# First batch of a fused agent-attention and expert layer: queries moved behind the values, 320 instead of 384 units checked per token

## The chip, the cores and the metric

The kernel runs on one core of one Trainium2 chip. The metric is the device time of one launch in microseconds (us). Engines are named as in the profile: PE is TensorE (PEld its weight loads), DVE is VectorE, ACT is ScalarE, POOL is GpSimd, SP is SyncE, which here only issues DMAs.

## What is computed

The reference, cut to what matters (B = 4 batches, N = 11456 tokens, 49 agents, width 128, E = 8 experts with 1024 hidden units):

```python
def sm(a, b):                         # softmax of scaled scores
    s = scale * (a @ b.transpose(0, 2, 1))
    e = np.exp(s - s.max(-1, keepdims=True))
    return e / (e.sum(-1, keepdims=True) + 1e-09)
agent_v = sm(agents, k) @ v           # 49 x 128 for each batch
x = (sm(q, agents) @ agent_v).reshape(B * N, 128)
...
expert_idx = argmax(normalized(x) @ normalized(expert_emb).T / tau)
gate_w = softmax probability of the chosen expert
for e in range(E):                    # tokens of expert e
    h = np.maximum(x[mask] @ w1[e], 0.0)
    out[mask] = gate_w[mask, None] * (h @ w2[e])
```

## The kernel before, in words

Each batch is cut into 12 units of 128 tokens by up to 8 (the last unit is 96 by 2). A unit of keys, values or queries is one DMA of 512 KB into a ring of 11 buffers (`unit_load`, L134 to L153). SP issues the loads in a fixed order, and load number n waits until the unit in load n-11 has been used.

For a batch b the work is:
- **keys** (`k1_f32`, L363): PE transposes the unit (tile `fTp`, `pe_T` L346), ACT and DVE copy it out (`fT`), PE multiplies by the agents (`sp`), ACT keeps the scores (`s_u`), DVE holds a running maximum (`m_run`).
- **maximum** (`k_max`, L416): one maximum over all tokens for each agent, by a transpose (`mT`), a reduction and a broadcast (`mB`, `pm`).
- **values** (`k2_unit`, L385): DVE subtracts the maximum, ACT takes the exponential (`kd`), PE multiplies with the values (`avp`), DVE adds up (`avx`).
- **the chain** (`av_chain` L421 and `pick_expert` L471): `foldp` and `avT` give agent_v; `key` and `e0i` choose the expert that most tokens of the batch will take; SP reads that number and loads its two weight matrices (`w1s`, `w2s`, `load_expert` L653); `gp` gives the product G of weights and agent_v, 1024 units by 49 agents. The units are ranked by how far their 49 numbers differ in sign (`diag`, in the trace written into `sel`; `row`; `rank`), and a selection matrix (`sel`) places the first 256 (384 in the last batch) into `gh` and `gl`.
- **queries** (`q_unit`, L666): PE transposes the unit, multiplies by the agents (`sp`), DVE and ACT form the exponentials (`qe`, `e`), which come back transposed (`tt`; for the first four units by PE as `tp`, later by DMA), then `rtp` gives routing scores (`rtg`, `rt`, `qq`), which `route_group` turns into gates.
- **the expert layer** (`ffn_mm1`, `ffn_mm2`): the 256 placed units get the full two-layer product (`hp`, `hh`, `hl`, `yp`). Of the other units the sign is held to be the same for all tokens, so that they enter as one linear map (`lin`).
- **the check** (`proved`, L810): the next `FVS[b]` units in rank are checked token by token with one matmul `vp`, whose least value is taken by DVE (`vmin`) or whose negative part is summed by ACT (`vsum`, L824). All units behind these are covered by a bound on the token alone. A token that fails, or that belongs to another expert, is a stray (`mark_strays`): up to 3 per partition and 128 per batch are computed again in one pass per batch (`fix`), what is left is handled in passes of a loop at the end (`stray`).

Ahead of the first expert product, `first()` (L1210) writes batch 0 out by hand. Its list `ops` is: 12 key units, query units 0 and 1, the maximum, then 12 value units, with query units 2 and 3 and key units 0 and 1 of batch 1 put between them (`BETWEEN`). Then come the chain up to `gl` and the rest. After that a table of ticks lays batch b's expert products over the keys, values and queries of the batches to come, and a scheduler orders each engine's instructions (SP's order is as written).

Of the kernel before, what the change touches and what calls it, by code (L numbers as in the profile page):

```python
# [10 lines left out]
F32 = mybir.dt.float32  # L11
# [3 lines left out]
ALU = mybir.AluOpType  # L15
# [3 lines left out]
P = 128  # L19
# [10 lines left out]
def kernel(ctx: ExitStack, tc: tile.TileContext, q, k, v, agents, emb, tau, w1, w2, out):  # L30
# [7 lines left out]
    NMS = [2] * (B - 1) + [3]  # L38
    FVS = [3 * P] * (B - 1) + [4 * P]
    FW = 4 * P  # L40
# [41 lines left out]
    def pss(name):  # L82
        return ps_s.tile([P, 512], F32, name=name, tag="s")
# [186 lines left out]
    def setup():  # L270
# [39 lines left out]
        yield 2  # L310
        t_ = pss("embT")
        pe.transpose(out=t_[:, :E], in_=emb_sb, identity=ident[:E, :E])
# [8 lines left out]

    y_last, h_last = [], []
    x_slots, s_slots, d_slots, e_slots, t_slots, qe_slots = slots(XB), slots(NU), slots(len(kds)), slots(len(e16)), slots(TB), slots(LEAD)
# [99 lines left out]
    def av_chain(b, g):  # L423
        bt = batches[b]
        while not ready:
            yield 1
        psx = pss if ffn_at[0] else psh
        s = psx("foldp")
# [22 lines left out]
        pe.matmul(out=rp[:, :E], lhsT=bt.avT, rhs=enT, start=True, stop=True)  # L451
        pe.matmul(out=rp[:, E + 1 : RW], lhsT=bt.avT, rhs=bt.avT[:, :A], start=True, stop=True)
        bt.sg, bt.isg = yield from half_scale(total(sq, psx), 7, "sg")
# [13 lines left out]
        yield 4  # L467
        s = pss("avsT")
        pe.transpose(out=s[:A, :D], in_=bt.avT[:, :A], identity=ident)
        act.copy(av_all[:, b, :], s[:A, :D])  # L470

    def pick_expert(b, g):
# [5 lines left out]
        def psx(name):  # L478
            return (pss if ffn_at[0] else psh)(name)

# [36 lines left out]
        def col(nm, dt=F32):  # L517
            return sm.tile([P, NF], dt, name=nm, tag=nm)
# [35 lines left out]
        act.copy(gs_[0], gg)  # L554
        vec.tensor_tensor(out=gs_[1], in0=gg, in1=gs_[0], op=ALU.subtract)
        gmx = sm.tile([P, 2], F32, name="gmx", tag="gmx")
        dve.tensor_reduce(out=gmx[:, :1], in_=ga, axis=AX.XY, op=ALU.max, apply_absolute_value=True)
        yield g
        for h in range(2):
# [4 lines left out]
            yield g  # L564

        rank, more = col("rank"), col("more")
        for c in range(NF // 2):
# [12 lines left out]
        def placed(h, w):  # L580
            t_ = psx("placed")[:, :w]
            for c in range(NF):
                pe.matmul(out=t_, lhsT=gt16[:, h, c].rearrange("p h a -> p (h a)"), rhs=sel[:, c, :w],
                          start=(c == 0), stop=(c == NF - 1))
            return t_

        act.copy(gh, placed(0, FM))
        yield g
        dve.tensor_copy(gl, placed(1, FM))
        bt.gh, bt.gl = gh, gl  # L590
        yield g
        act.activation(w2x[:, :, 0], w2s, AF.Square, accum_out=sq[1])
# [73 lines left out]
    def q_unit(b, u, g):  # L666
# [6 lines left out]
        i = yield from take(x_slots)  # L673
        xT = pe_T(units["q", b, u], p, n)
        used("q", b, u)
# [528 lines left out]

    QF = 2
    BETWEEN = {1: ("q", 0, 2), 5: ("q", 0, 3), 8: ("k", 1, 0), 11: ("k", 1, 1)}
    NEXT = sum(x[0] == "k" for x in BETWEEN.values()) if B > 1 else 0
    AHEAD = LB - 2

    def first():  # L1210

        ops = [("k", 0, u) for u in range(NU)] + [("q", 0, u) for u in range(QF)] + [("m", 0, 0)]
        for u in range(NU):
            ops.append(("v", 0, u))
            if u in BETWEEN and BETWEEN[u][1] < B:
                ops.append(BETWEEN[u])
        X = {"k": k, "v": v, "q": q}
        loads = [o for o in ops if o[0] in X]
        li = 0
        q0 = []  # L1220
        for kind, b, u in ops:
            if kind in X:
                li += 1
                for o in loads[: li + AHEAD]:
                    while o not in units and len(ring) >= LB and ring[-LB][1] is None:
                        yield 1
                    unit_load(X[o[0]], *o)
            if kind == "k":
                if not hasattr(batches[b], "blks"):
                    k_start(b)  # L1230
                spawn(k1_f32(b, u))
            elif kind == "v":
                spawn(k2_unit(b, u, dve, (0, 1)))
            elif kind == "q":
                g = q_unit(b, u, (1, 0, 0, 1, 0) if u < QF else (1, 1, 1, 5, 1))
                if u == 0:
                    q0.append(g)
                    spawn(iter(lambda: next(q0[0]), None))
                else:
                    spawn(g)  # L1240
            else:
                kb = batches[0].blks[0]
                while kb.k1 < len(kb.us):
                    yield 1
                with tc.high_priority():
                    now_run(k_max(0, psh, 0))
            yield 1
        while batches[0].blks[0].k2 < NU or not ready:
            yield 1
        with tc.high_priority():  # L1250
            now_run(av_chain(0, 0))
            now_run(q0[0])
            q0[0] = iter(())
            while not hasattr(batches[0], "gl"):
                next(batches[0].pick)
        yield from batches[0].pick

# [156 lines left out]
```

## Time and profile before

| what | value |
|---|---|
| median of 3 runs | 865.67 us (864.28 to 867.6) |
| the profiled execution, own time | 861.1 us |
| its span | 859.3 us |
| mean granted TensorE clock | 0.939 of full speed |
| busy: PE, DVE, ACT, POOL | 90%, 74%, 55%, 35% |
| loaded and stored | 114.5 MB, mean 133 GB/s |

The profiled execution lies 4.6 us under the median of the runs. Its span runs from the first instruction to the last; 1.8 us of its time lie outside. The granted clock is shown as a share of full speed: 1.00 is 2.4 GHz and 0.50 is 1.2 GHz. A matmul of float32 operands leaves two records in the trace for each one in the program; a transpose leaves one.

### The profile page before, as it was taken

The numbers are of one execution on the slowest core, as the hardware profiler recorded it, in microseconds if no ns is written. First come the engines' busy times: TensorE is split into PE (matmuls) and PEld (weight loads), VectorE is DVE, ScalarE is ACT, GpSimd is POOL, SyncE is SP. The second block draws the span as 40 slices with busy tenths as digits, with TensorE's granted clock in tenths as the row PEclk, the third lists the DMA queues.
The fourth block names the chain that finished last, engine by engine and source line by source line (L and its number), as shares of the span: only waits on it lengthen the run. The fifth ranks groups of instructions, "written<-read, shape, count | busy, mean of one in ns | idle before, by whom it ended". The sixth has DMA issues, their size and how long they took to land. (4 is left out here: it accounts for less than half of the span.)

```text
span 859.3 us, 20983 instructions
## 1 busy us (share of the span) xinstructions
PE 771.5 (90%) x8158; PEld 647.7 (75%) x8158; DVE 636.1 (74%) x1576; ACT 475.7 (55%) x1191; POOL 303.8 (35%) x554
## 2 busy tenths in 40 slices
PE   8979469999998889989998979989995779999986
PEld 6978359988787687868987768878883657888765
DVE  5545586786666997967578976967686979887976
ACT  2434254675655835665557624766557436776662
POOL 4000221334603353553414353544522634334420
PEclk9969569999998999999999979999998989999998
DMA  8737106456417145855537143764342224521311
GB/s 332 216 103 263 58 1 214 136 154 207 146 60 241 71 116 153 250 167 159 184 76 224 46 132 104 210 186 132 88 132 56 75 56 109 150 79 42 101 46 57
DMA packets 126608, 114.50 MB, mean 133 GB/s; under 512 B 47541, under 2 KB 102921, under 8 KB 126507
## 3 DMA queue, kind: packets, MB, share of 16 engines
q1 hardware_dynamic: 113131, 89.58, 36.2%
q10 hardware_dynamic: 13120, 23.47, 7.4%
q8 instruction: 65, 1.06, 0.5%
q14 instruction: 36, 0.29, 0.1%
q0 software_dynamic: 256, 0.10, 0.1%
HBM read 79.14 MB, written 23.72 MB: 120 GB/s over the span
## 5 line engine op out<-in xcount | busy, mean ns | idle before, releaser
L941 DVE SCALAR_TENSOR_TENSOR hl<-hp,hh 128x512 f16<-128x512 f32 (+1 forms) x207 | 137.6, 668 | 40.9 <-ACT hh L940 40.1
L940 ACT ACTIVATE hh<-hp 128x512 f16<-128x512 f32 (+1 forms) x207 | 120.1, 584 | 82.6 <-PE hp L937 73.7
L824 ACT ACTIVATE vp<-vp,la 128x384 f32<-128x384 f32 (+1 forms) x224 | 130.1, 581 | 51.7 <-PE vp L821 34.3
L964 PE MATMUL yp<-w2p,hh 128*128 128x128 f16 (+1 forms) x810 | 154.9, 220 | 0.4 <-ACT hh L940 0.4
L965 PE MATMUL yp<-w2p,hh 128*128 128x128 f16 (+1 forms) x810 | 154.9, 220 | 0.0
L966 PE MATMUL yp<-w2p,hl 128*128 128x128 f16 (+1 forms) x810 | 151.2, 220 | 1.4 <-DVE hiv L216 1.0
L821 PE MATMUL vp<-vm,tt 128*128 128x384 f16 (+1 forms) x360 | 115.2, 342 | 6.9 <-ACT vp L824 2.8
L679 PEld LDWEIGHTS sp<-aT_all,fT 128*128 128x128 f32 x720 | 89.4, 196 | 7.9 <-issue 1.8
L964 PEld LDWEIGHTS <-hh 128*128 128x128 f16 (+1 forms) x810 | 81.3, 100 | 17.9 <-issue 1.4
L679 PE MATMUL sp<-aT_all,fT 128*128 128x49 f32 x720 | 91.1, 276 | 3.5 <-DVE hsc L212 1.4
L376 PEld LDWEIGHTS sp<-aT_all,fT 128*128 128x128 f32 x720 | 89.4, 196 | 5.0 <-DVE lin L615 2.4
L376 PE MATMUL sp<-aT_all,fT 128*128 128x49 f32 x720 | 90.1, 274 | 2.5 <-DVE lin L615 2.2
L966 PEld LDWEIGHTS <-hl 128*128 128x128 f16 (+1 forms) x810 | 79.8, 99 | 14.5 <-issue 2.5
L826 DVE TENSOR_REDUCE vmin<-vp 128x1 f32<-128x384 f32 (+3 forms) x136 | 78.7, 580 | 14.9 <-PE vp L821 14.5
L936 PE MATMUL hp<-tt,gh 128*128 128x512 f16 (+1 forms) x207 | 77.9, 376 | 10.4 <-ACT vp L824 8.1
L965 PEld LDWEIGHTS <-hh 128*128 128x128 f16 (+1 forms) x810 | 80.3, 99 | 8.5 <-issue 1.4
L358 DVE COPY fT<-fTp 128x512 f32<-128x512 f32 x88 | 60.0, 684 | 24.9 <-PE fTp L355 24.5
L937 PE MATMUL hp<-tt,gl 128*128 128x512 f16 (+1 forms) x207 | 78.0, 377 | 0.0
L360 ACT COPY fT<-fTp 128x512 f32<-128x512 f32 (+1 forms) x96 | 54.0, 564 | 29.5 <-PE fTp L355 29.4
L694 POOL TENSOR_TENSOR e<-qe,e 128x392 f16<-128x392 f32 (+1 forms) x44 | 38.0, 864 | 89.7 <-ACT e L693 88.6
L955 PE MATMUL yp<-lin,tt 128*128 128x128 f16 x720 | 66.5, 220 | 2.8 <-DVE ot L979 2.7
L773 POOL TENSOR_TENSOR nrm<-qq,half 128x16 f32<-128x16 f32 (+2 forms) x28 | 68.5, 2446 | 0.2
(330 smaller groups left out, 1644.8 us busy)
## 6 DMA issues: line engine op xcount, KB each, us to landing
kt<-in_k_dram SPq DMA_DIRECT2D x44, 512.0 KB, 5.9
qt<-in_q_dram SPq DMA_DIRECT2D x44, 512.0 KB, 4.4
vt<-in_v_dram SPq DMA_DIRECT2D x44, 512.0 KB, 4.9
out_dram<-ot ACTq DMA_DIRECT2D x88, 256.0 KB, 2.6
w1s<-in_moe_w_dram SPq DMA_DIRECT2D x8, 512.0 KB, 3.7
w2s<-in_moe_w_dram SPq DMA_DIRECT2D x8, 512.0 KB, 5.3
tt<-e SPq DMA_TRANSPOSE x44, 3.1
kt<-in_k_dram SPq DMA_DIRECT2D x4, 96.0 KB, 6.0
```

The source lines that it names most:

```text
L376: pe.matmul(out=s[:p, c * A : (c + 1) * A], lhsT=kT[:, c * p : (c + 1) * p], rhs=aT_all[:, b, :], start=True, stop=True)
L679: pe.matmul(out=s[:p, c * A : (c + 1) * A], lhsT=xT[:, c * p : (c + 1) * p], rhs=aT_all[:, b, :], start=True, stop=True)
L821: pe.matmul(out=z[:p, :FV], lhsT=tts[b, u][:, c * p : (c + 1) * p], rhs=bt.vm, start=True, stop=True)
L824: act.activation(z[:p, :FV], z[:p, :FV], AF.Relu, bias=bt.l[:p, at], scale=-1.0, accum_out=bt.vsum[:p, at])
L826: dve.tensor_reduce(out=bt.vmin[:p, at], in_=z[:p, :FV], axis=AX.X, op=ALU.min)
L936: pe.matmul(out=hp[:, :m], lhsT=bt.gh[:, fs], rhs=tt, start=True, stop=False)
L937: pe.matmul(out=hp[:, :m], lhsT=bt.gl[:, fs], rhs=tt, start=False, stop=True)
L940: h_last[:] = [act.activation(hh[:, :m], hp[:, :m], AF.Relu)]
L941: dve.scalar_tensor_tensor(out=hl[:, :m], in0=hp[:, :m], scalar=0.0, in1=hh[:, :m], op0=ALU.max, op1=ALU.subtract)
L964: pe.matmul(out=y, lhsT=hh[:, cs], rhs=wh, start=False, stop=False, skip_group_check=True)
L965: pe.matmul(out=y, lhsT=hh[:, cs], rhs=wl, start=False, stop=False, skip_group_check=True)
L966: y_last[:] = [pe.matmul(out=y, lhsT=hl[:, cs], rhs=wh, start=False, stop=last, skip_group_check=True)]
```

## The change

The first batch's order is now: 12 key units, maximum, 12 value units, the chain as far as `rp`; queries 0 and 1 are put behind `rp` on PE, queries 2 and 3 behind the start of the chain's second half. Batch 1's key units 0 and 1 go to the general plan (`NEXT = 0`). The chain's small products of batch 0 use the two output banks (`psy`) instead of the four hidden-layer banks. The maximum `gmx` and the low half `gs_[1]` are written later. In batches 0 to 2 the check covers 320 units and not 384.

```diff
-    FVS = [3 * P] * (B - 1) + [4 * P]
+    FVS = [P * 5 // 2] * (B - 1) + [4 * P]
...
-        t_ = pss("embT")
+        t_ = psy("embT")
...
-        psx = pss if ffn_at[0] else psh
+        psx = pss if ffn_at[0] else psy
...
-        pe.matmul(out=rp[:, E + 1 : RW], lhsT=bt.avT, rhs=bt.avT[:, :A], start=True, stop=True)
+        i = pe.matmul(out=rp[:, E + 1 : RW], lhsT=bt.avT, rhs=bt.avT[:, :A], start=True, stop=True)
+        if not ffn_at[0]:
+            p_last.append(i)
...
-        s = pss("avsT")
+        s = psx("avsT")
...
-        vec.tensor_tensor(out=gs_[1], in0=gg, in1=gs_[0], op=ALU.subtract)
-        gmx = sm.tile([P, 2], F32, name="gmx", tag="gmx")
-        dve.tensor_reduce(out=gmx[:, :1], in_=ga, axis=AX.XY, op=ALU.max, apply_absolute_value=True)
...
+        vec.tensor_tensor(out=gs_[1], in0=gg, in1=gs_[0], op=ALU.subtract)
         rank, more = col("rank"), col("more")
...
         bt.gh, bt.gl = gh, gl
+        dve.tensor_reduce(out=gmx[:, :1], in_=ga, axis=AX.XY, op=ALU.max, apply_absolute_value=True)
...
-        xT = pe_T(units["q", b, u], p, n)
+        with in_place(p_last):
+            xT = pe_T(units["q", b, u], p, n)
...
-    QF = 2
-    BETWEEN = {1: ("q", 0, 2), 5: ("q", 0, 3), 8: ("k", 1, 0), 11: ("k", 1, 1)}
-    NEXT = sum(x[0] == "k" for x in BETWEEN.values()) if B > 1 else 0
+    NEXT = 0
...
-        ops = [("k", 0, u) for u in range(NU)] + [("q", 0, u) for u in range(QF)] + [("m", 0, 0)]
...
+        k_start(0)
         for u in range(NU):
...
+            yield from fetch(u + 1 + AHEAD)
+            spawn(k1_f32(0, u))
+            yield 1
+        while batches[0].blks[0].k1 < NU:
+            yield 1
+        with tc.high_priority():
+            now_run(k_max(0, psy, 0))
+        for u in range(NU):
+            yield from fetch(NU + u + 1 + AHEAD)
+            spawn(k2_unit(0, u, dve, (0, 1)))
+            yield 1
+        yield from fetch(len(loads))
         while batches[0].blks[0].k2 < NU or not ready:
             yield 1
         with tc.high_priority():
             now_run(av_chain(0, 0))
-            now_run(q0[0])
-            q0[0] = iter(())
+        for u in range(2):
+            spawn(q_unit(0, u, (1, 0, 0, 1, 0)))
+        while len(tts) < 2:
+            yield 1
+        p_last.clear()
+        with tc.high_priority():
             while not hasattr(batches[0], "gl"):
                 next(batches[0].pick)
+        for u in range(2, LEAD):
+            spawn(q_unit(0, u, (1, 0, 0, 1, 0)))
         yield from batches[0].pick
```

Line numbers of the changed kernel differ by 2 or 3 from those of the kernel before (L562 becomes L561, L679 becomes L682, L715 becomes L718).

How the engines' order moves, at three places. First, PE from the last unit of keys to the first values (`qt` is a query unit, `vt` a value unit, `m` the running maximum). Before:

```order
L376 MATMUL sp<-aT_all,fT 96x49 x2
L679 MATMUL sp<-aT_all,fT 128x49 x8
...
L355 MATMUL fTp<-ident,qt 128x128 x5
L196 MATMUL mT<-ident,m_582 49x128
L355 MATMUL fTp<-ident,qt 128x128 x3
L679 MATMUL sp<-aT_all,fT 128x49 x4
L201 MATMUL mB<-ident,mTx 128x49
L679 MATMUL sp<-aT_all,fT 128x49 x4
L405 MATMUL avp<-vt,kd_152 64x129 x8
```

Now:

```order
L376 MATMUL sp<-aT_all,fT 96x49 x2
L196 MATMUL mT<-ident,m_527 49x128
L201 MATMUL mB<-ident,mTx 128x49
L312 MATMUL embT<-ident,emb_sb 128x8
L405 MATMUL avp<-vt,kd_152 64x129 x8
```

The two query units that stood around the maximum are gone from this place, and the values follow it directly; between the values, too, only `avp` is left.

Second, PE from the fold of the values to the ranking product `row` (left out are the transposes `tp` and the pairs `rtp`, 16 and 32 matmuls now, 16 `rtp` before). Before:

```order
L376 MATMUL sp<-aT_all,fT 128x49 x8
L431 MATMUL foldp<-fold,avx 128x49
...
L451 MATMUL rp<-enT,avT 128x8
L452 MATMUL rp<-avT 128x49
L222 MATMUL total<-avsq,ones 128x1
...
L522 MATMUL gp<-avT,w1s 128x49 x8
L222 MATMUL total<-wsq_1022,ones 128x1
L562 MATMUL row<-sel,ones 128x512 x2
```

Now:

```order
L451 MATMUL rp<-enT,avT 128x8
L452 MATMUL rp<-avT 128x49
L355 MATMUL fTp<-ident,qt 128x128 x16
L222 MATMUL total<-avsq,ones 128x1
L682 MATMUL sp<-aT_all,fT 128x49 x12
L471 MATMUL avsT<-ident,avT 49x128
L682 MATMUL sp<-aT_all,fT 128x49 x4
L524 MATMUL gp<-avT,w1s 128x49 x8
...
L355 MATMUL fTp<-ident,qt 128x128 x12
...
L682 MATMUL sp<-aT_all,fT 128x49 x12
L561 MATMUL row<-sel,ones 128x512 x2
```

The last eight `sp` of batch 1's keys no longer stand ahead of `foldp`; two query units stand between `rp` and `gp`, two more between `gp` and `row`.

Third, DVE between the mean of G and the matrix `diag` (written into `sel`) that `row` waits for. Before:

```order
L533 TENSOR_REDUCE mean<-gts 128x8
...
L536 TENSOR_REDUCE pw<-sel 128x8
...
L555 TENSOR_TENSOR gt_158<-gts,gt_158 128x16x49
L538 TENSOR_SCALAR pw<-pw 128x8
...
L550 TENSOR_TENSOR sel<-ident,key 128x1024
```

Now:

```order
L565 TENSOR_TENSOR gt_158<-gts,gt_158 128x16x49
L736 TENSOR_TENSOR rt<-rtp,qe 128x392
L542 RECIPROCAL pw<-pw 128x8
L772 TENSOR_REDUCE rmx<-rtg 128x8
L739 TENSOR_REDUCE qq<-rt 128x2x8
L358 COPY fT<-fTp 128x512
L544 TENSOR_TENSOR key<-key,pw 128x8
L736 TENSOR_TENSOR rt<-rtp,qe 128x392
L546 TENSOR_SCALAR key<-key 128x8
L739 TENSOR_REDUCE qq<-rt 128x2x8
...
L552 TENSOR_TENSOR sel<-ident,key 128x1024
```

Routing work of queries 0 and 1 and copies for queries 2 and 3 now stand between the steps of `key`.

## Rows read from the trace of the kernel before

**Rows 1.** Windows of the whole core. Columns: stretch in us, its length, busy us (and instructions) of PE, PEld, DVE, ACT, POOL, then granted clock, DMA share, GB/s.

```profile
20.00:42.00 22.00, 22.00 (x205) 22.00 (x205) 11.40 (x34) 8.64 (x18) 0.68 (x6) 1.00 0.74 218
50.00:60.00 10.00, 10.00 (x64) 9.32 (x61) 4.88 (x10) 4.78 (x9) 0.11 (x1) 0.50 0.26 65
68.00:86.00 18.00, 17.00 (x209) 15.19 (x205) 9.44 (x23) 7.90 (x15) 0.00 (x0) 0.99 0.86 290
96.00:117.00 21.00, 7.56 (x23) 4.98 (x24) 11.81 (x36) 10.07 (x18) 4.07 (x8) 0.50 0.01 3
124.00:800.00 676.00, 629.55 (x6859) 527.88 (x6859) 521.43 (x1246) 400.58 (x1031) 269.73 (x462) 0.97 0.45 133
```

**Rows 2.** The timeline from the last keys to the first values. Columns here and in the next three groups: start us, duration us, engine, line, operation, tile written <- tiles read, shapes, count of merged records, and in brackets the idle time before and what ended it.

```profile
41.96 0.46 PE L376 MATMUL sp<-aT_all,fT 128*96 128x49 f32 x4
43.72 0.82 DVE L419 TENSOR_REDUCE m<-m_run 128x49 f32<-128x392 f32 x1
51.30 0.42 PE L196 MATMUL mT<-ident,m 128*49 128x128 f32 x1
51.76 0.28 DVE L198 TENSOR_REDUCE mTx<-mT 49x1 f32<-49x128 f32 x1 [2.41 <-PE mT L196]
53.90 0.66 PE L201 MATMUL mB<-ident,mTx 49*128 49x49 f32 x2
55.44 1.48 ACT L399 ACTIVATE kd<-kd 128x392 f32<-128x392 f32 x3 [0.63 <-DVE kd L396]
56.36 3.71 PE L405 MATMUL avp<-vt,kd 128*64 128x129 f32 x32
```

**Rows 3.** The timeline: the same PE work at either clock, and the end of the values.

```profile
51.52 0.85 PE L355 MATMUL fTp<-ident,qt 128*128 128x128 f32 x3
52.16 1.81 PE L679 MATMUL sp<-aT_all,fT 128*128 128x49 f32 x8
63.05 1.99 PE L679 MATMUL sp<-aT_all,fT 128*128 128x49 f32 x16 [0.85 <-ACT fT L360]
125.34 1.06 PE L355 MATMUL fTp<-ident,kt 128*128 128x128 f32 x8
73.92 1.10 PE L405 MATMUL avp<-vt,kd 128*64 128x129 f32 x16
83.02 1.33 PE L405 MATMUL avp<-vt,kd 128*64 128x129 f32 x20 [0.19 <-issue]
```

**Rows 4.** The timeline of the chain from the fold to the sum of squares of the first weights.

```profile
86.40 0.39 PE L431 MATMUL foldp<-fold,avx 128*128 128x49 f32 x2
87.28 0.56 DVE L346 TENSOR_TENSOR m_run<-sp,m_run 128x392 f32<-128x392 f32 x1
89.67 0.64 PE L452 MATMUL rp<-avT 128*128 128x49 f32 x2
91.70 0.36 SPq L658 DMA_DIRECT2D w1s<-in_moe_w_dram  x1
95.51 3.65 PE L522 MATMUL gp<-avT,w1s 128*128 128x49 f32 x16 [2.27 <-DMA w1s<-in_moe_w_dram]
98.96 0.55 PE L222 MATMUL total<-wsq,ones 128*128 128x1 f32 x2
```

**Rows 5.** The timeline of the chain's second half, up to the first expert product, and query steps that now stand in it (the transposed copy `tt`, `rt`, `qq`).

```profile
106.52 3.75 PE L562 MATMUL row<-sel,ones 128*128 128x512 f32 x4 [7.01 <-DVE nkey L552]
110.93 1.28 DVE L568 TENSOR_SCALAR_CACHE_REDUCE sel<-sel,key 128x1024 f16<-128x1024 f32 x1 [4.47 <-ACT sel L563]
116.11 0.16 DVE L573 TENSOR_SCALAR rank<-more 128x4 f32<-128x4 f32 x1
121.64 0.41 DVE L589 CAST gl<-placed 128x256 f16<-128x256 f32 x1
124.09 0.38 PE L936 MATMUL hp<-tt,gh 128*128 128x512 f16 x1 [0.24 <-ACT fT L360]
50.48 1.01 ACT L700 COPY tt<-tp 128x1024 f16<-128x1024 f16 x1 [1.86 <-PE tp L699]
93.53 0.57 DVE L733 TENSOR_TENSOR rt<-rtp,qe 128x392 f32<-128x392 f32 x1 [1.22 <-ACT rtg L731]
94.20 0.97 DVE L736 TENSOR_REDUCE qq<-rt 128x16 f32<-128x784 f32 x1
52.40 0.69 DVE L358 COPY fT<-fTp 128x512 f32<-128x512 f32 x1 [0.36 <-PE fTp L355]
```

**Rows 6.** Groups of instructions by line with different shapes apart, whole span: count, busy us, mean ns of one, idle before. The check's matmul and ACT's pass over it.

```profile
L821 PE MATMUL vp<-vm,tt 128*128 128x384 f16 x264 | 80.6, 329 | 5.1 <-DVE vmin L826 2.2 <-ACT vp L824 1.8 <-DVE hl L941 0.8
L821 PE MATMUL vp<-vm,tt 128*128 128x512 f16 x88 | 31.9, 385 | 1.6 <-ACT vp L824 1.0 <-ACT vm L645 0.4
L824 ACT ACTIVATE vp<-vp,la 128x384 f32<-128x384 f32 x165 | 91.5, 555 | 37.9 <-PE vp L821 26.6 <-POOL la L805 8.8 <-PE yp L966 0.6
L824 ACT ACTIVATE vp<-vp,la 128x512 f32<-128x512 f32 x55 | 36.4, 661 | 9.4 <-PE vp L821 6.4 <-PE mB L201 2.4 <-POOL la L805 0.2
```

**Rows 7.** A window where batch 0's expert products end and batch 1's begin, columns as in rows 1.

```profile
290.00:300.00 10.00, 7.73 (x91) 6.28 (x90) 10.00 (x21) 7.94 (x21) 3.09 (x8) 1.00 0.07 26
```

**Rows 8.** The passes over strays: the writes of their answers (nanoseconds; first and last start in us), and the start of the pass that the last one ends.

```profile
L1075 POOL DMA_INDIRECT out_dram<-so,ix x4: 1114/1127/1131, 429.8 to 853.6; - x4
800.46 0.23 DVE L1101 TENSOR_SCALAR_CACHE_REDUCE ind<-cum,it 128x32 f32<-128x32 f32 x1
```

More of the change, by code (lines that the diff above doesn't have):

```diff
@@ L317 @@
     ready = []
-    y_last, h_last = [], []
+    y_last, h_last, p_last = [], [], []
     x_slots, s_slots, d_slots, e_slots, t_slots, qe_slots = slots(XB), slots(NU), slots(len(kds)), slots(len(e16)), slots(TB), slots(LEAD)
@@ L478, in psx @@
         def psx(name):
-            return (pss if ffn_at[0] else psh)(name)
+            return (pss if ffn_at[0] else psy)(name)
         sav = sm.tile([P, 1], F32, name="sav", tag="sav")
@@ L585, in placed @@
             return t_
+        gmx = sm.tile([P, 2], F32, name="gmx", tag="gmx")
         act.copy(gh, placed(0, FM))
@@ L1201, in run_step @@
         run_half()
-    QF = 2
-    BETWEEN = {1: ("q", 0, 2), 5: ("q", 0, 3), 8: ("k", 1, 0), 11: ("k", 1, 1)}
-    NEXT = sum(x[0] == "k" for x in BETWEEN.values()) if B > 1 else 0
+    NEXT = 0
     AHEAD = LB - 2
     def first():
-        ops = [("k", 0, u) for u in range(NU)] + [("q", 0, u) for u in range(QF)] + [("m", 0, 0)]
-        for u in range(NU):
[L1214 to L1246, printed above, removed]
-            yield 1
@@ new lines, in first, with fetch @@
+        X = {"k": k, "v": v, "q": q}
+        more = [("q", 0, u) for u in range(LEAD)]
+        loads = [(x, 0, u) for x in "kv" for u in range(NU)] + more
+        def fetch(n):
+            for o in loads[:n]:
+                while o not in units and len(ring) >= LB and ring[-LB][1] is None:
+                    yield 1
+                unit_load(X[o[0]], *o)
+        k_start(0)
+        for u in range(NU):
+            yield from fetch(u + 1 + AHEAD)
+            spawn(k1_f32(0, u))
+            yield 1
```

## The prediction

> **What bounds the kernel now.** I read the windows of the whole core first, then the timeline of the first 125 us, then the groups by line. From 124 to 800 us PE is busy 629.55 of 676 us at a clock of 0.97 [rows 1]: there the kernel is bound by PE, and work taken off PE is worth nearly its own length. Before that it is not. From 96 to 117 us PE works 7.56 of 21 us, at 0.50; from 50 to 60 us it is busy all the time, but also at 0.50 [rows 1]. The first expert product `hp` starts at 124.09 [rows 5]. Everything ahead of it is a path of single steps: keys, maximum, values, fold, choice of the expert, its weights, G, ranks, placement. Three views show where that path waits for other work. First, the keys' last product ends at 42.42 (41.96 + 0.46) and the maximum is reduced at 44.54, yet the first value product starts only at 56.36 [rows 2], because query units 0 and 1 stand in PE's order around `mT` and `mB`. Second, the values take from 56.36 to 84.35 (83.02 + 1.33), 28.0 us [rows 2, 3], although a unit takes PE 1.86 us at half clock (3.71 for two) and 1.10 at full [rows 2, 3]; queries 2 and 3 and keys of batch 1 stand between. Third, `gp` starts at 95.51 when its weights land, 3.8 us after their issue [rows 4], and PE does little until `row` at 106.52 [rows 5].
>
> **The change, step by step** (times on the profiled execution's clock; F is the start of the fold, G the end of the second `total`).
>
> *Keys to values.* Query 0's eight transposes leave the keys' stretch: 1.06 us [rows 3], so the keys end at 41.4. From there: 2.12 to the end of the reduction, 0.74 from `mT` to its maximum (51.30 to 52.04), 2.03 from `mB` to the first exponential (53.90 to 55.93, a third of 1.48 behind 55.44) [rows 2]. Sum 46.3: the values start 10.1 us earlier.
>
> *Values.* 90 columns are 11.25 units of eight. All at full clock 12.4 us, all at half 20.9. DVE is no limit: it was busy 9.44 of 18 us in the densest stretch, 68 to 86 us [rows 1]. The clock will be low at the start, since PE has little to do for 5 us before; in the stretch from 68 to 86 us, with values in it, it was 0.99. I take three units at half (5.6) and 8.25 at full with a little gap (9.2): 14.8 us, end at 61.1, F = 61.4 where it was 86.40 [rows 4]. That is 25.0 us earlier; with the bounds, F lies between 59.0 and 67.5. The last eight `sp` of batch 1's keys, which stood right ahead of the old fold, are out of its way too; this is in the 25.0.
>
> *Fold to G.* Here the change gives time back. `rp` ended at F + 3.9 [rows 4]; without the key unit's `m_run` (0.56 [rows 4]) on DVE it ends at F + 3.35. Then PE has two query units in its order before `gp`: 16 transposes, 32 records of `sp`, the first `total` and `avsT`. At full clock that is 2.1 (twice 1.06) + 4.0 (twice 1.99) + 0.6 = 6.7 us, at half 4.5 (16 of 0.28) + 7.2 (32 records at 1.81 for eight) + 0.9 = 12.6 us [rows 3]. So `gp` starts between F + 10.1 and F + 16; it was F + 9.1. I take the middle, F + 13, because the same mix of transposes and `sp` ran at 1.00 from 20 to 42 us and at 0.50, with PE never idle, from 50 to 60 us [rows 1]. The Trainium skill ("TensorE: Matmul & The Clock Gate", section "What's actually happening") holds that the low clock is the resting state and that a busy PE releases it; read plainly, values and queries would all run at full clock, which makes the sum 839 (a rival below) instead of 848.5. The row from 50 to 60 us speaks against so plain a reading.
>
> The weights are no longer what `gp` waits for. SP issues 11 loads of 512 KB as values 1 to 11 are used, from about 50 us. At the 290 GB/s of the densest stretch [rows 1] each takes 1.8 us, so that they end near 70 and `w1s`, queued behind them, lands near 72: F + 10.5, inside the queries' time. `gp` and `total` took 4.0 us at 0.50 (95.51 to 99.51) [rows 1, 4]; I take 3.3, as the clock may have risen. G = F + 16.3 = 77.7, was 99.51: 21.8 us are left of 25.0. Bounds 71.4 and 87.5.
>
> *G to the first `hp`.* It was 24.6 us (99.51 to 124.09). On DVE, `rt`, `qq` and a copy `fT` for each of two queries now stand ahead of `diag`: 2 x (0.57 + 0.97 + 0.69) = 4.5 us. On ACT two copies `tt` of 1.01 stand around G's scaling: 1.7 of the 2.0 on the path. During the ranks (110.93 to 116.11) ACT gets two more such copies and two casts of about 0.5: +3.0. A `rt` and a `fT` stand in the placement: +1.3. Off the path goes the wait from `gl`'s end, 122.05, to `hp`, 2.0, filled by query 4's transposes, which now come earlier [rows 5]. PE, fed with queries, should have a better clock than the 0.50 of before: `row` alone took 3.75 [rows 5], so half of it and of the placement may go; I take -3.0. Sum +5.5, so `hp` is at G + 30.1 = 107.8, 16.3 us earlier. From below the step is +0.1 (all clock gained, ACT's copies hidden), from above +12.9 (no clock gained, query 3's `sp` late ahead of `row`): `hp` between 96 and 125.
>
> *Moved, not saved.* Keys 0 and 1 of batch 1 go where PE is full: 2 x (1.06 + 1.99) = 6.1 [rows 3]; query 4's `sp`, 1.0, comes ahead of `hp` in exchange. +5.1. Nothing covers it.
>
> *The check.* 264 matmuls `vp` go from 384 to 320 columns. The rows give 329 ns at 384 and 385 at 512 [rows 6], 28 ns for 64 columns: 7.4 us of PE. ACT's 165 passes shorten by 53 ns, 8.7 us [rows 6]. Where batches change, DVE is at 10.00 of 10 and PE at 7.73 [rows 7], and PE's saving is lost. I take 6.0, between 3 (half lost there) and 9 (where ACT's passes held PE up).
>
> *Strays.* Fewer units checked one by one means that the bound on the token has to cover more. From the reference's own inputs I worked out both criteria: 72, 47 and 21 tokens fail in batches 0 to 2 (44, 29 and 11 with 384), never more than 3 in a partition nor 128 in a batch. So the one pass for each batch still takes them all, and no pass is added to the four of before [rows 8]: 0. The other edits (`psy`, `gmx`, `gs_[1]`) move names of banks and 0.5 us steps that DVE's order has in the same places: 0.
>
> *Sum.* 861.1 - 16.3 + 5.1 - 6.0 = 843.9 against the profiled execution. That one is 4.6 us under the median of the runs, so **848.5** for a median, 2.0% faster.
>
> **The rivals.**
>
> *Full clock.* PE, never waiting between values and queries, runs at 1.00: F = 59.0, G = F + 12.4, `hp` 27 later at 98.4, 25.7 earlier: 834.5, as a median 839. For it speaks 68 to 86 us, against it 50 to 60 us [rows 1]. The Trainium skill's section on the clock, named above, read plainly, would have it so.
>
> *Half clock and a clogged chain.* All values at half (F = 67.5), the queries ahead of `gp` at half (G = F + 20), `hp` 31 later at 118.5: only 5.6 gained. With +5.1 and -5.0 that is 855.6, as a median 860. The row of 50 to 60 us speaks for it; 68 to 86 against.
>
> *A repair pass too many: slower.* It decides at the fourth failing token of one partition in a batch. Batches 0 and 1 have three, so a single token that the device's rounding flags and mine does not would do. Then the loop at the end runs once. The last pass of before took from 800.46 to past 853.6 [rows 8], 54 us beside other work; alone I take half to three quarters of that, 27 to 40 us: near 885. Against it: it takes one token in just the wrong partition.
>
> *The gain is lost at the first change of batches.* Twelve key units of batch 1 must fit where ten did, its maximum and values come late, and its chain is late for batch 0's end. The delay is those two units' 6 us again, up to twice that: 855 to 862.
>
> **How the numbers follow.** Forecast 0.55, full clock 0.17, half clock 0.17, late batch 0.07, repair pass 0.04. A measurement of this kernel tells about 0.5%, 4.3 us, from no change. All of the forecast and the full clock are faster than that, two thirds of the half clock and half of the late batch: 0.87. The rest of these two is within it: 0.09. Slower 0.04. The range goes from 835, inside the full-clock case, to 862, behind the half-clock case. It leaves out the repair pass and the tails of the two clocks.
>
> **What would show it.** Right: first `avp` near 46, fold near 61, `gp` behind the queries' `sp` and not ended by a DMA, first `hp` near 108, and from there to the end some 734 us where it was 735. Wrong: values slower than 1.5 us a unit, `row` waiting for PE's queries and not for DVE, `hp` after 118, or more than four answers written for strays. If `hp` is early and the end is not, the step that failed is the one on the moved keys or on the check.

## The result, and the profile after

The changed kernel takes 837.9 us (median of 4 runs, 837.3 to 841.2) beside 865.0 us before (4 runs, 857.8 to 867.6): ratio 0.971, interval 0.964 to 0.977. A second measurement, beside the kernel before again, gave 836.6 us (6 runs, 828.4 to 840.9), ratio 0.969 (0.964 to 0.975). The prediction said 848.5 us, 835 to 862, faster. The sign and the range held, and the gain is about 10 us larger than forecast. The profiled execution took 837.4 us, span 835.6, mean clock 0.947.

Windows of the changed kernel, columns as in [rows 1]:

```profile
46.00:52.00 6.00, 5.77 (x68) 5.80 (x70) 2.75 (x7) 2.14 (x5) 0.12 (x1) 0.63 0.22 45
52.00:62.00 10.00, 8.10 (x127) 7.73 (x123) 6.62 (x21) 3.69 (x9) 0.00 (x0) 0.94 1.00 378
62.00:68.00 6.00, 6.00 (x30) 6.00 (x30) 2.78 (x13) 1.74 (x4) 0.00 (x0) 0.50 1.02 408
68.00:74.00 6.00, 6.00 (x31) 6.00 (x30) 2.04 (x5) 2.37 (x5) 0.84 (x1) 0.50 0.74 252
78.00:104.00 26.00, 20.39 (x187) 17.65 (x188) 23.16 (x60) 15.82 (x31) 7.99 (x17) 0.81 0.01 2
104.00:820.00 716.00, 665.44 (x7296) 559.89 (x7295) 552.60 (x1359) 422.44 (x1102) 281.56 (x485) 0.96 0.46 131
```

The values run mostly at full clock (52 to 62), the two query units ahead of `gp` at half clock with PE never idle (62 to 74), and in the chain's second half DVE is busy 23.16 of 26 us. Behind 104 us PE is the fullest engine, as before.

Chosen rows of the timeline of the same kernel, from the last keys to the first `hp`. They answer to [rows 2, 4, 5]:

```profile
42.40 0.81 DVE L419 TENSOR_REDUCE m<-m_run 128x49 f32<-128x392 f32 x1
43.27 0.31 PE L196 MATMUL mT<-ident,m 128*49 128x128 f32 x1 [2.05 <-DVE m L419]
46.23 12.20 PE L405 MATMUL avp<-vt,kd 128*64 128x129 f32 x180 [1.41 <-issue]
54.71 0.29 DVE L413 TENSOR_TENSOR avx<-avp,avx 128x129 f32<-128x129 f32 x1
55.59 0.29 DVE L413 TENSOR_TENSOR avx<-avp,avx 128x129 f32<-128x129 f32 x1
58.99 0.42 PE L431 MATMUL foldp<-fold,avx 128*128 128x49 f32 x2 [0.56 <-DVE avx L413]
61.84 0.64 PE L452 MATMUL rp<-avT 128*128 128x49 f32 x2
62.29 3.64 PE L355 MATMUL fTp<-ident,qt 128*128 128x128 f32 x16
63.45 0.36 SPq L660 DMA_DIRECT2D w1s<-in_moe_w_dram  x1
66.00 5.33 PE L682 MATMUL sp<-aT_all,fT 128*128 128x49 f32 x24
69.38 1.06 ACT L525 ACTIVATE sel<-w1s 128x1024 f16<-128x1024 f32 x1 [1.57 <-DMA w1s<-in_moe_w_dram]
72.93 3.61 PE L524 MATMUL gp<-avT,w1s 128*128 128x49 f32 x16
76.35 0.55 PE L222 MATMUL total<-wsq,ones 128*128 128x1 f32 x2
87.90 1.22 DVE L552 TENSOR_TENSOR sel<-ident,key 128x1024 f32<-128x1024 f32 x1
89.19 1.98 PE L561 MATMUL row<-sel,ones 128*128 128x512 f32 x4 [0.24 <-DVE sel L552]
91.87 1.28 DVE L568 TENSOR_SCALAR_CACHE_REDUCE sel<-sel,key 128x1024 f16<-128x1024 f32 x1 [0.58 <-ACT sel L562]
99.47 0.17 DVE L573 TENSOR_SCALAR rank<-more 128x4 f32<-128x4 f32 x1 [0.45 <-ACT sel L570]
101.58 0.41 DVE L590 CAST gl<-placed 128x256 f16<-128x256 f32 x1
103.27 0.38 PE L939 MATMUL hp<-tt,gh 128*128 128x512 f16 x1
```

`hp` starts 20.8 us earlier than in [rows 5]. `gp` follows the queries' `sp` with no wait; its weights are there at 69.38, when ACT reads them. This holds for this execution and not for every one (see the rivals below).

Groups of instructions, shapes apart, which answer to [rows 6], and the writes of the strays' answers, to [rows 8]:

```profile
L824 PE MATMUL vp<-vm,tt 128*128 128x320 f16 x264 | 73.5, 305 | 4.9 <-ACT vp L827 2.0 <-DVE vmin L829 1.9 <-DVE hl L944 0.6
L827 ACT ACTIVATE vp<-vp,la 128x320 f32<-128x320 f32 x165 | 82.7, 501 | 35.4 <-PE vp L824 23.8 <-POOL la L808 5.4 <-DVE ot L982 2.9
L829 DVE TENSOR_REDUCE vmin<-vp 128x1 f32<-128x320 f32 x99 | 47.4, 482 | 17.0 <-PE vp L824 16.5
L1078 POOL DMA_INDIRECT out_dram<-so,ix x4: 1114/1126/1132, 415.0 to 830.7; - x4
```

The row of `vmin` in the kernel before:

```profile
L826 DVE TENSOR_REDUCE vmin<-vp 128x1 f32<-128x384 f32 x99 | 54.0, 548 | 14.1 <-PE vp L821 13.9
```

The check became shorter on three engines: PE 80.6 to 73.5 us, ACT 91.5 to 82.7, DVE's `vmin` 54.0 to 47.4. The strays still take four passes.

The rest is best read by batches. When the copy `gh` of a batch starts, its expert products follow. The starts of `gh` (from the timelines of ACT) and the end of the span, in us, and the four stretches between:

| kernel | `gh` of batch 0, 1, 2, 3 | end | stretches |
|---|---|---|---|
| before | 121.1, 304.3, 488.9, 673.2 | 859.3 | 183.2, 184.6, 184.4, 186.1 |
| before, 320 checked | 121.1, 301.3, 487.4, 668.2 | 851.2 | 180.2, 186.1, 180.8, 183.0 |
| changed | 101.3, 288.9, 474.2, 652.1 | 835.6 | 187.6, 185.3, 177.9, 183.5 |
| changed, second | 98.1, 283.9, 467.9, 649.3 | 832.5 | 185.8, 184.0, 181.3, 183.2 |
| changed, 384 checked | 98.9, 287.6, 472.6, 653.0 | 835.9 | 188.8, 185.0, 180.4, 182.9 |
| the same, second | 96.6, 285.2, 470.4, 660.5 | 844.8 | 188.6, 185.2, 190.2, 184.3 |
| keys put back | 109.0, 291.1, 478.0, 659.1 | 843.7 | 182.1, 186.9, 181.0, 184.6 |

One stretch differs by up to 10 us between two executions of the same program (180.4 and 190.2). So a few us in the rest can be read only where several rows agree.

### The profile page after: what moved, and what is told of

Read it like the earlier page. It is cut to its first block, busy times and chain, and to the rows that moved or that the text cites. A ratio compares the mean times of both kernels' runs of the same rounds, so it can differ in the third digit from the quotient of the medians.

```text
span 835.6 us, 20995 instructions
## 1 busy us (share of the span) xinstructions
PE 762.4 (91%) x8158; PEld 648.5 (78%) x8158; DVE 626.0 (75%) x1576; ACT 466.3 (56%) x1191; POOL 303.5 (36%) x554
## 5 line engine op out<-in xcount | busy, mean ns | idle before, releaser
L943 ACT ACTIVATE hh<-hp 128x512 f16<-128x512 f32 (+1 forms) x207 | 120.3, 585 | 80.6 <-PE hp L940 67.6
L969 PE MATMUL yp<-w2p,hl 128*128 128x128 f16 (+1 forms) x810 | 153.8, 221 | 1.4 <-DVE hl L944 1.4
L827 ACT ACTIVATE vp<-vp,la 128x320 f32<-128x320 f32 (+1 forms) x224 | 121.3, 541 | 45.6 <-PE vp L824 29.5
L824 PE MATMUL vp<-vm,tt 128*128 128x320 f16 (+1 forms) x360 | 107.5, 324 | 6.7 <-ACT vp L827 3.4
L682 PEld LDWEIGHTS sp<-aT_all,fT 128*128 128x128 f32 x720 | 90.5, 198 | 4.8 <-DVE hsc L212 0.7
L682 PE MATMUL sp<-aT_all,fT 128*128 128x49 f32 x720 | 91.6, 278 | 0.8 <-DVE hsc L212 0.5
L968 PEld LDWEIGHTS <-hh 128*128 128x128 f16 (+1 forms) x810 | 81.1, 100 | 6.6 <-issue 0.7
L829 DVE TENSOR_REDUCE vmin<-vp 128x1 f32<-128x320 f32 (+3 forms) x136 | 71.8, 530 | 17.4 <-PE vp L824 16.7
```

Of the source, the lines that this page charges most:

```text
L682: pe.matmul(out=s[:p, c * A : (c + 1) * A], lhsT=xT[:, c * p : (c + 1) * p], rhs=aT_all[:, b, :], start=True, stop=True)
L824: pe.matmul(out=z[:p, :FV], lhsT=tts[b, u][:, c * p : (c + 1) * p], rhs=bt.vm, start=True, stop=True)
L827: act.activation(z[:p, :FV], z[:p, :FV], AF.Relu, bias=bt.l[:p, at], scale=-1.0, accum_out=bt.vsum[:p, at])
L943: h_last[:] = [act.activation(hh[:, :m], hp[:, :m], AF.Relu)]
L968: pe.matmul(out=y, lhsT=hh[:, cs], rhs=wl, start=False, stop=False, skip_group_check=True)
L969: y_last[:] = [pe.matmul(out=y, lhsT=hl[:, cs], rhs=wh, start=False, stop=last, skip_group_check=True)]
```

## The experiments

**The two halves of the change, each alone.** In the changed kernel 384 units are checked again; in the kernel before, 320.

```diff
-    FVS = [P * 5 // 2] * (B - 1) + [4 * P]
+    FVS = [3 * P] * (B - 1) + [4 * P]
```

> The changed kernel with 384 units checked in batches 0 to 2, as before. Theory (the check's matmuls are paid where PE is full): first hp unchanged at 103 to 104 us, and 6 us more behind it, so about 844 where the changed kernel gave 837.9. Rival (the check hides behind other engines, the whole gain is the first batch's order): 838 to 839.

Measured 843.6 us (837.8 to 848.1), ratio to before 0.985 (0.979 to 0.992), as the theory said for the total.

> The kernel before with 320 units checked in batches 0 to 2, nothing else. Theory: first hp stays at 124 us, the rest loses 6 us, about 859 against 865 of before. Rival (the check hides): 864 to 866. Rival (other stalls at the batch changes shrink too): 855.

Measured 851.4 us (846.5 to 854.2, and one run of 1881.5 that the ratio leaves out), ratio 0.990 (0.985 to 0.994). So the order alone is worth some 1.5%, the check alone 1.0%, about 8.8 us. Together that is 2.5%, inside the interval of the whole, 2.3 to 3.6%. As the changed kernel was not measured beside these two, it ran again beside the first:

> The changed kernel with 384 units checked in batches 0 to 2, once more, beside the changed kernel on the same chip. Theory: the check's 64 columns are worth 6 us (3 to 9) in the new order as in the old: total 843 to 847 if the changed kernel shows 838. Rival: in the new order the ticks hide them, and the two lie within 3 us of each other.

> The changed kernel itself once more, for a comparison on one chip with the runs beside it: 836 to 841 us, ratio to the kernel before 0.965 to 0.977 by the theory that the first measurement stands; a rival, that the chip of the first measurement was favourable, gives 0.978 to 0.985.

Measured 847.5 us (842.8 to 849.5), ratio 0.983 (0.979 to 0.987), and for the changed kernel 836.6, ratio 0.969. The check is worth 1.4% there, with the intervals 6 to 18 us; the medians lie 10.9 us apart, more than the 3 to 9 expected. It is not hidden in the new order. `hp`, expected at 103 to 104 us with 384 checked, came at 100.9 and 98.6; why is said with the rivals below.

**The moved keys.** Batch 1's keys 0 and 1 stand between the values again.

```diff
-    NEXT = 0
+    NEXT = 2
...
+            if u in (8, 11):
...
+                spawn(k1_f32(1, (u - 8) // 3))
...
```

> The changed kernel with batch 1's key units 0 and 1 put back among the first batch's values (behind value units 8 and 11), all queries still behind the values. Theory (work moved from the values to a stage where PE is full is not saved, only paid later): fold and first hp some 5 to 6 us later, near 109, and the rest 6 us shorter, total 836 to 840. Rival (keys in the ticks cost more than their own length, since they delay batch 1's chain): total 830 to 834. Rival (they hide in the ticks): 843.

Measured 844.8 us (842.6 to 847.0), ratio 0.985 (0.980 to 0.990); fold at 65.6, `hp` at 112.1. The total lies above all three that were expected. From `hp` to the end it takes 731.6 us where the changed kernel takes 732.3, which looked as if the keys cost nothing in the ticks. The table by batches tells more: the stretch of batch 0, where they lie, has 182.1 us with the keys put back and 180.2 in the kernel before with the same check, but 187.6 and 185.8 with them moved. That is 4 to 7 us. At 384 it is 183.2 against 188.8 and 188.6. To the end this does not stay: from batch 0's `gh` on, the kernel before with 320 takes 730.1 us, the changed one 734.3 and 734.4, and this one 734.7, though it has the keys in front. So the price shows in the stretch of batch 0, and whether all of it reaches the total is not shown.

**The queries' place.** All four query units between the values, with the keys still in the ticks. This is not the order of before, where units 0 and 1 stood around the maximum, and 2 and 3 took their steps further apart:

```diff
+            if u in (1, 3, 5, 7):
...
+                spawn(q_unit(0, u // 2, (1, 0, 0, 1, 0)))
...
-        for u in range(2):
-            spawn(q_unit(0, u, (1, 0, 0, 1, 0)))
...
```

> The changed kernel with queries 0 to 3 put back among the first batch's values; the keys of batch 1 stay in the ticks, and the maximum still follows the keys directly. Theory (query work beside the chain is covered in part, among the values it is not): fold 11 to 13 us later, near 71, gp again ended by its weights at fold + 9, first hp near 107, total near 841. Rival (queries clog the chain by as much as they free the values): first hp 103, total 838. Rival (the gain of the change came from the queries' place altogether): first hp 115 or later, total 850.

Measured 855.5 us (853.7 to 859.7), ratio 0.998 (0.996 to 1.000): the gain is gone, although the check is still the shorter one; with that check the order of before had 851.4 in the same round, so this place of the queries is worse than the old one. The last rival came nearest, with `hp` at 117.4. The fold came at 81.1, 22 us later, 21 of them between the first `avp` (47.33) and the fold. Chosen rows of this kernel's timeline around one query unit show why it costs more than its work:

```profile
53.90 0.28 DVE L413 TENSOR_TENSOR avx<-avp,avx 128x129 f32<-128x129 f32 x1
54.24 1.10 PE L405 MATMUL avp<-vt,kd 128*64 128x129 f32 x16 [0.43 <-DVE avx L413]
55.95 0.62 PE L702 MATMUL tp<-ident,e 128*128 128x128 f16 x8 [0.61 <-DVE e L697]
56.41 1.04 PE L355 MATMUL fTp<-ident,qt 128*128 128x128 f32 x8
58.58 1.99 PE L682 MATMUL sp<-aT_all,fT 128*128 128x49 f32 x16 [1.13 <-ACT fT L360]
60.49 3.55 PE L405 MATMUL avp<-vt,kd 128*64 128x129 f32 x32
```

The next `avp` stands behind `sp` in PE's order, and `sp` waits for the copies `fT`, which start only when the transposes are done. From 55.34 (54.24 + 1.10) to 60.57 PE works 3.5 of 5.2 us. From the first `avp` to the fold it is busy 27.6 of 33.8 us, where the changed kernel has 12.2 of 12.8: of the 21 us more, 15.4 are work, mostly the queries' own, and 5.6 are waits. `avp` itself takes 15.0 us and not 12.2, since some units now stand alone (1.10 each). Moving the queries away took out these waits, too.

**Queries behind `gp`.** The opposite step: units 0 and 1 follow `gp`.

```diff
-        if not ffn_at[0]:
-            p_last.append(i)
...
+        if b == 0:
+            p_last.append(i)
...
+            while not p_last:
+                next(batches[0].pick)
```

> The changed kernel with queries 0 and 1 behind gp in PE's order instead of ahead of it. Theory (PE's order, not the weights, holds gp back by the 3.5 us between the landing at 69.4 and its start at 72.9): gp at fold + 10.4 to 10.8, G 3 us earlier, but both query units then stand ahead of the ranks, first hp between 102 and 106, total 836 to 841. Rival (what counts is only when gp starts): first hp near 100, total 834.

Measured 853.9 us (847.9 to 855.9), ratio 0.986 (0.977 to 0.995). Theory and rival were both wrong. A window and the rows of `gp` and `hp`:

```profile
68.00:74.00 6.00, 0.31 (x2) 0.34 (x2) 0.00 (x0) 0.42 (x1) 0.00 (x0) 0.50 0.83 297
```

```profile
73.69 3.62 PE L522 MATMUL gp<-avT,w1s 128*128 128x49 f32 x16 [7.94 <-DMA w1s<-in_moe_w_dram]
115.78 0.63 PE L939 MATMUL hp<-tt,gh 128*128 128x512 f16 x1
```

PE stands still until the weights land, 11.8 us behind the fold (61.86), so `gp` comes only 2 us sooner behind it than in the changed kernel (13.9); then all the query work stands in the second half, and `hp` is 12.5 us later. Some 3.0 us of that are not the edit's: this profiled execution, and those of the next two experiments, began the keys late, because DVE's first steps (L175, which no edit touches) took 6.79 us and not 0.97. At the maximum `mT` 3.0 us of it are left here (46.23 for 43.27), 1.8 and 2.3 in the next two; the cause is open, and so is whether the runs without a profile had it. From the fold, `hp` is 9.6 us later. The queries ahead of `gp` fill a wait that is there anyway.

**PE's clock.** 21 products of zeros (128x512) behind the last keys, `mB` and the fold; they write a bank that nothing reads.

```diff
+        fill(9, "k")
         with tc.high_priority():
             now_run(k_max(0, psy, 0))
+        fill(6, "mB")
...
```

> The changed kernel with 21 matmuls of zeros (128x512 float16, 0.21 us each at full clock, results unused) on PE while it waits: nine behind the last keys, six behind mB, six behind the fold. Theory (the low clock after each wait is a cost of its own): values start at full clock, 12.2 us become about 10.5, and the queries and gp behind the fold run at full clock, G 4 to 5 us earlier, then gp is ended by its weights; first hp near 98, total 832 to 834. Rival (the clock does not follow so short a filling): values 12 us, 0.50 behind the fold, total 838 to 840, the fillers' own length hidden or 1 us paid.

Measured 838.7 us (837.4 to 843.2), ratio 0.972 (0.964 to 0.981). Windows of this kernel:

```profile
52.00:62.00 10.00, 9.40 (x131) 8.19 (x127) 6.63 (x23) 3.41 (x10) 0.00 (x0) 1.00 1.00 370
62.00:68.00 6.00, 4.81 (x45) 4.69 (x43) 4.46 (x13) 2.20 (x6) 0.84 (x1) 0.96 1.03 410
68.00:74.00 6.00, 4.51 (x25) 4.54 (x26) 1.02 (x6) 2.79 (x5) 0.20 (x1) 0.50 0.74 251
```

The clock was indeed high to 68 us: `avp` took 10.1 us and not 12.2, and G ended at 73.5 instead of 76.9. But `gp` (69.49) now waited 2.68 us for its weights, and `hp` came at 105.9, 2.6 us later, of which 1.8 lie ahead of the maximum. Behind G it lost 6.0 us: `row` started 14.9 us behind G and not 12.3, as `qmx` and `qe` of queries 2 and 3, ready sooner, now stood ahead of `diag` on DVE, and from `row` to `hp` it took 17.5 us and not 14.1, with `row` itself at 3.50 and not 1.98. So the better clock ahead of G gained nothing in the total here. (In the second execution of the changed kernel, below, it did bring `hp` forward.)

**DVE's share.** Two experiments take work off DVE. In the first, every third value unit's subtraction runs on POOL; in the second, the low half of the query exponentials.

```diff
-            spawn(k2_unit(0, u, dve, (0, 1)))
+            spawn(k2_unit(0, u, pool if u % 3 == 2 else dve, (0, 1)))
```

> The changed kernel with every third of the first batch's twelve value units subtracted on POOL (0.95 us each) and not on DVE (0.56). Theory (at full clock the values go at DVE's pace: 0.29 + 0.56 is 0.85 of the 0.88 us that a unit takes): 0.6 to 1.5 us off the values' 12.2, total 837. Rival (PE's own stream of 16 passes is the 0.88): values 12.2 or a little more because POOL is slower, total 838 to 839.

Measured 840.1 us (839.2 to 841.6), ratio 0.972 (0.964 to 0.980); values in 12.3 us as before. They started 2.4 us later, but 2.3 of that was there at the maximum already, ahead of any subtraction:

```profile
45.53 0.45 PE L196 MATMUL mT<-ident,m 128*49 128x128 f32 x1 [2.04 <-DVE m L419]
```

So the theory that DVE sets the pace of the values finds no support, and the rival stands.

```diff
-        (dve if f32 else pool).tensor_tensor(out=e2[:p, :n, LO : LO + A], in0=e, in1=hi, op=ALU.subtract)
+        pool.tensor_tensor(out=e2[:p, :n, LO : LO + A], in0=e, in1=hi, op=ALU.subtract)
```

> The changed kernel, but the low half of the exponentials of query units 0 to 3 is subtracted on POOL and not on DVE. Theory: the stretch from G to the first hp (26.4 us in the changed kernel) is set by DVE's order, because query steps stand ahead of the matrix diag and of the ranks; with two subtractions fewer on DVE ahead of diag it ends 1 to 3 us earlier: hp at 100 to 102 us instead of 103.3, total 835 to 837 us against 837.9. Rival: PE's clock or POOL's latency sets it, and nothing moves: hp at 103 or later, total 838 to 840.

Measured 839.5 us (837.4 to 847.1), ratio 0.975 (0.971 to 0.980); `hp` at 103.8. The timelines of this kernel, and of the second execution of the changed one, where the clock ahead of G was alike (1.00 from 62 to 68 us in both):

```profile
72.91 0.55 PE L222 MATMUL total<-wsq,ones 128*128 128x1 f32 x2
81.97 1.22 DVE L552 TENSOR_TENSOR sel<-ident,key 128x1024 f32<-128x1024 f32 x1
85.99 1.95 PE L561 MATMUL row<-sel,ones 128*128 128x512 f32 x4
```

```profile
72.54 0.55 PE L222 MATMUL total<-wsq,ones 128*128 128x1 f32 x2
84.10 1.22 DVE L552 TENSOR_TENSOR sel<-ident,key 128x1024 f32<-128x1024 f32 x1
85.38 1.98 PE L561 MATMUL row<-sel,ones 128*128 128x512 f32 x4 [0.24 <-DVE sel L552]
```

`diag` is 2.5 us earlier behind G, so DVE's order did hold it. But `row` then waits for PE instead, which is full of queries 2 and 3 at a low clock (6.00 of 6 us at 0.67 from 80 to 86, where the second execution had 5.07 at 1.00), and starts 12.5 us behind G beside 12.3. From `row` to `hp` it takes 17.8 us beside 14.3: `rank` is there at 95.75, but query 3's `tp` (97.71) and the next unit's transposes stand ahead of the last `placed` (100.27) on PE. The low half itself takes 0.91 us on POOL for 0.57 on DVE. So the first half of the theory holds, and the rival holds for the total; the clock and POOL's longer steps changed together, and what each cost is not shown.

**Fewer queries in the chain.** Only query units 0 and 1 stay; 2 and 3 go to the general plan.

```diff
-    LEAD = min(4, NU)
+    LEAD = 2
+    QE = 4
...
```

> The changed kernel, but only query units 0 and 1 are put into the chain; 2 and 3 go to the general plan behind the first hp. Theory: behind hp PE is the bound and work costs its own length, ahead of it the second half of the chain is bound by DVE and ACT, which lose the steps of two query units: hp at 95 to 99 us (4 to 8 earlier), the rest longer by the 6 us of PE work that moves there, so total within 3 us of 837.9. Rival 1: the ticks have room, as they had for the keys of batch 1: the rest grows by under 2 us and the total is 831 to 834. Rival 2: the late queries hold up the first expert products, rest longer by over 8 us, total over 841.

Measured 871.3 us (870.4 to 871.8), ratio 1.011 (1.007 to 1.014). The second rival was right on the total, but not on the place. `hp` is earlier, at 100.2, and the stretch of batch 0 is no longer than before (186.2). The loss comes far behind: the stretch of batch 1 takes 211.4 us. The timelines of the chain of batch 2, of this kernel and of the changed one:

```profile
430.66 0.37 PE L432 MATMUL foldp<-fold,avx 128*128 128x49 f32 x2
454.70 0.36 PE L487 MATMUL key<-enT,sav 128*128 128x8 f32 x2 [0.79 <-DVE qe L690]
457.51 0.36 SPq L661 DMA_DIRECT2D w1s<-in_moe_w_dram  x1
```

```profile
427.33 0.37 PE L431 MATMUL foldp<-fold,avx 128*128 128x49 f32 x2
436.38 0.34 PE L486 MATMUL key<-enT,sav 128*128 128x8 f32 x2
439.08 0.35 SPq L660 DMA_DIRECT2D w1s<-in_moe_w_dram  x1
```

With the queries two units later in the table, `key`, which chooses the expert, stands 24 us behind the fold in PE's order and not 9. Its weights are issued 18 us later, and the expert products of batch 2 start 23 us later. In batch 3 the weights are issued 21 us behind the fold, and not 11.

**A repair pass more.** One slot less for strays in a partition makes tokens fall to the loop at the end.

```diff
-    KEEP = 3
+    KEEP = 2
```

> The changed kernel with room for 2 failing tokens in a partition and not 3, which prices the rival of the prediction: batches 0 and 1 have partitions with 3, so two passes are added in the loop at the end. Theory: each takes 27 to 40 us alone, total 892 to 918, and six answers are written instead of four. Rival (a pass costs what the last one took beside other work, 54 us): 946. Rival (the device finds fewer failing tokens than I worked out): 838.

Measured 882.1 us (878.6 to 885.7), ratio 1.019 (1.011 to 1.028), with two passes more:

```profile
L1078 POOL DMA_INDIRECT out_dram<-so,ix x6: 1012/1110/1129, 413.8 to 879.6; - x6
```

(882.1 - 837.9) / 2 = 22 us each: under my 27 to 40, but more than the gain of the order, 1.5% or 13 us. The count of three in a partition mattered.

## Why the prediction was right, and where its sizes were off

*Keys to values.* Right: first `avp` at 46.23, predicted 46.3. The path without the queries was the sum of its rows.

*Values.* Mis-sized: 12.8 us to the fold for the 15.1 taken. The three units at half clock were there, and took 5.0 us (5.6 taken). But units at full clock follow each other 0.88 us apart (54.71 and 55.59 above); the 1.10 of [rows 3] is that of one unit alone, from its first start to its last end. The fold came at 58.99, at the lower bound, which stood for all units at full clock and 1.10 each: that the two agree is luck.

*Fold to G.* Right in its mechanism for this execution: the queries' `sp` end it, not the weights, which were there 10.4 us behind the fold (10.5 predicted). G came at 76.9 = F + 17.9, for F + 16.3. `gp` started at F + 13.9, near the F + 13 taken, but not for the reason given: all of the query work ran at half clock, for which the sum had F + 16. It came 2 us below that because the prices were too high (16 transposes took 3.64 us, not 4.5). The rest is `gp` and `total`, 4.0 us for 3.3, at half clock, too.

*G to `hp`.* Mis-sized, 26.4 us for 30.1. From G to `row` 12.3 us, where it was 7.0: +5.3, I had +6.2. The ranks, from their first step to `rank`, 7.6 for 5.2: +2.4, I had +3.0. The other two pieces, `row` to the ranks and `rank` to `hp`, gave 1.7 and 4.2 back: -5.9, for which I had -3.7 (+1.3 - 2.0 - 3.0). So the clock under `row` and the placement was worth more than taken: `row` took 1.98 instead of 3.75, and the clock granted from 98 to 104 us was 0.98.

*Moved keys.* Right where they lie: +5.1 predicted, about 5.5 in the stretch of batch 0 (188.7 for 183.2, both at 384). That it is paid to the end is not shown (the experiment above).

*The check.* Too small: 6.0 with 3 to 9; measured 8.8 and, in the new order, 1.4% of some 860, about 12, each uncertain by 4 to 6. I priced the longer of PE's and ACT's saving with a discount for the places where DVE is full. But `vmin` on DVE was shortened as well, by 66 ns 99 times, and that term I did not have. That the saving of all three engines makes up the larger value fits, but is not shown apart.

*Strays and the other edits.* Right: four passes. `gmx` and the low half of G (`gt`) start on DVE ahead of `diag` as before (80.39 and 82.11; 101.74 and 102.94 before), so 0 was right for their place. No run takes the edit of the banks (`psy`) back alone.

*Sum.* The profiled executions differ by 23.7 us, predicted 17.2: 4.5 of the missing 6.5 lie ahead of `hp` (2.4 in the values, -1.6 to G, 3.7 behind it), 2.0 after it. The other 4 us of the 10.6 are that the profile of before lay below its median, and that of after does not.

*The rivals.* The full clock was no separate case: the changed kernel does both. In the second execution, F is 57.95 and the stretch that ran at 0.50 runs so:

```profile
62.00:68.00 6.00, 4.35 (x41) 4.22 (x39) 4.30 (x13) 1.15 (x3) 0.00 (x0) 1.00 1.04 396
```

```profile
69.29 3.45 PE L524 MATMUL gp<-avT,w1s 128*128 128x49 f32 x16 [2.94 <-DMA w1s<-in_moe_w_dram]
99.71 0.38 PE L939 MATMUL hp<-tt,gh 128*128 128x512 f16 x1
```

There the weights bind `gp` after all, at F + 11.3, which that rival had overlooked, and `hp` is only 3.6 us earlier. This is no rare case: of the eight profiled executions with this order up to `gp`, five (this one, both with 384 checked, POOL's low half, and fewer queries in the chain) have `gp` waiting 2.3 to 3.8 us for `w1s`, and three do not. In the five the clock from 62 to 68 us was 0.78 to 1.00, in the three 0.50, 0.50 and 0.77. So the prediction's sign "not ended by a DMA" came true with the low clock of its execution. Half clock in all of the values, the late batch and the repair pass did not occur.

## What to carry to other kernels

Work that is put between the steps of a serial path costs more than its length, since each of its waits becomes one of the path; look instead for a stretch where the path waits for a transfer, as the queries found ahead of `gp`. Read a repeated unit's price from its spacing in a dense stretch, not from one that stands alone. When a check or a copy shrinks, price it on every engine that touches it, and before work is moved into a table, look at what its later entries delay: the experiment with fewer queries in the chain lost 33 us, some 340 us behind the edit.

## What the runs showed of the hardware

PE was busy 12.00 of 12 us from 62 to 74 us, right behind a stretch at 0.94, and yet was granted 0.50; a second execution of the same program had 1.00 from 62 to 68. From 67 to 71 us of the first only `sp` ran, 4.00 of 4 us, also at 0.50, while transposes and `sp` together had 1.00 from 20 to 42 us in [rows 1]. So a clock taken from one stretch does not tell that of another with the same work. The Trainium skill ("TensorE: Matmul & The Clock Gate", section "What's actually happening") says that activity releases the throttle and that its timing does not start with the kernel. The second half fits the two executions; the first, read as a rule that a PE without idle time runs at full clock, does not, as little as in the stretch from 50 to 60 us of [rows 1].
